# A cosformer attention and Sinkhorn-routed experts kernel: another order for the first batch, the second and third batch's attention, and the loads and transposes

## The chip, the cores and the metric

The kernel runs on one core of a Trainium2 chip. The metric is the device time of one execution in microseconds. Three executions of the kernel before took 971.24, 970.00 and 970.04 us, so the median is 970.04 us. The one that was profiled is the first of them.

The core has a matrix engine (PE; its weight loads are listed as PEld), a vector engine (DVE), a scalar engine (ACT), a general engine (POOL), and SP, which here only issues DMAs. Each engine works through its own list in order. DMAs are issued by POOL (loads that change float32 to float16 on the way) and by SP (transposes and the saved sums).

## The reference

Attention with cosine weights on 8 batches of 8 heads, 576 positions, head size 64, and then 8 experts on the 4608 rows that this gives:

```python
q_p = phi(q, cos_w, sin_w)              # relu, times cos and times sin, side by side
k_p = phi(k, cos_w, sin_w)
kv = einsum('bhsf,bhsd->bhfd', k_p, v)  # per head: features x head size
z = sum(k_p, axis=2)
num = einsum('bhsf,bhfd->bhsd', q_p, kv)
den = einsum('bhsf,bhf->bhs', q_p, z)[..., None] + 1e-06
x = (num / den) as 4608 rows of 512

P = exp(x @ w_gate - max)
for _ in range(8):                      # Sinkhorn
    P /= P.sum(1) + 1e-09; P /= P.sum(0) + 1e-09; P *= N / E
for e in range(8):
    out += P[:, e:e+1] * (relu(x @ w1[e]) @ w2[e])
```

## The kernel before, in words

The program has two phases. The second phase (expert 0's last tiles with the Sinkhorn iterations between them, then experts 1 to 7 by a scheme of seven products on quarter matrices) is the same in both kernels. The change lies in the first phase, which computes attention for all 8 batches and, interleaved with it, expert 0's two layers for the first 7 blocks of 512 rows.

**Order.** The lists of PE, DVE and ACT are written out by hand: te, ve and se are wrappers that tie each instruction behind the last one of the same engine. So an instruction that waits holds all that stand behind it. A block j has 16 slots: slots 0 to 7 are layer 1 (`ffn1`, one group of four matmuls of 512 columns and a relu on ACT each), slots 8 to 15 are layer 2 (`ffn2`, four matmuls each; every second one ends with a copy to the accumulators). `at(j, slot, fn, ...)` hangs a step of attention behind a slot. In block j these are the steps that finish batch b = j + 1 and those that prepare batch b + 1.

**Steps of a batch**, each for hk = 0 to 3 (two heads at a time):

- `load(b, half, names)`: POOL issues one load of 288 KB per name and half (two hk). The pool `ld` has 4 buffers a name, so two batches fit.
- `prep_q`: DVE's relu (from batch 2 on) and product with cos and sin give q_p, in a buffer of `qp_pool`. From batch 2 on SP then issues a DMA transpose of q_p into q_pT. For batches 0 and 1 `turn` transposes on PE by matmuls with the identity, and ACT or DVE moves the result out of PSUM with a relu.
- `prep_k` (relu on ACT or DVE), `prep_kp` (product with cos and sin on DVE), `prep_v` (copy of v next to a column of ones, on DVE or ACT); `prep_kv` is the last two.
- `sums(b, half)`: 36 small matmuls give kv and the key sums z for two hk, then ACT copies kv out and DVE writes `zsel`. Batch 0 gets its key sums apart, by `key_sums`, before the products k_p are there.
- `denominators(b)`: 24 matmuls of q_pT with zsel, then on DVE reciprocal, hi and hl.
- `spread_out(b, hk)`: three matmuls spread hl over the partitions, ACT copies them out as rb. `numerators(b, hk)`: four matmuls, and DVE's product with rb gives xT, the rows that the experts read. `attend` is both. The four PSUM banks of `small_ps` are shared by turns, sums, spread_out and numerators.
- `gates(b)`: 16 or 20 small matmuls and an exponential on ACT.

**Gates of the DMAs.** A load with `held_back` waits for the last DVE instruction that stands in the program before it; with `behind=(b, hk)` it waits instead for the transpose of that batch and hk to land. In the other direction the transposes of batches 3 and 4 wait for the landing of the first half of v of their batch, those of batches 5 to 7 for the second half of k.

**The start.** While the first loads land PE runs matmuls on constants (`idle_ps`), and `keep_busy(n)` puts n x 128 columns more of them between the steps of batch 0. Batch 0's steps are written out in order by hand; with their last ones layer 1's first four groups (`first_l1`) are interleaved by k-tile.

Of the kernel before, what the change touches and what calls it, by code (L numbers as in the profile page):

```python
# [10 lines left out]
FP32 = mybir.dt.float32  # L11
# [14 lines left out]
def kernel(  # L26
# [185 lines left out]
    with ExitStack() as p1:  # L212
        ld = p1.enter_context(tc.tile_pool(name="ld", bufs=4))
        kp_pool = p1.enter_context(tc.tile_pool(name="kp_pool", bufs=4))
        qp_pool = p1.enter_context(tc.tile_pool(name="qp_pool", bufs=4))
        qT_pool = p1.enter_context(tc.tile_pool(name="qT_pool", bufs=1))
        kv_pool = p1.enter_context(tc.tile_pool(name="kv_pool", bufs=2))
        rb_pool = p1.enter_context(tc.tile_pool(name="rb_pool", bufs=3))
# [8 lines left out]
        turnings = {}  # L227
        sources = {"q": q, "k": k, "v": v}

        def load(b, half, names="qkv", held_back=False, behind=None):  # L230
            for name in names:
                x = ld.tile([P, 2, C, D], F16, name=f"{name}_ld")
                view = sources[name][b].rearrange("(hk hh) (p c) d -> (hh p) hk (c d)", hh=2, c=C)
                i = nc.gpsimd.dma_start(
                    out=x[:].rearrange("p hk c d -> p hk (c d)"),
                    in_=view[:, 2 * half : 2 * half + 2],
                )
                if behind is not None:

                    after(turnings[behind], i)  # L240
                elif held_back:

                    after(ve.last, i)
                landing[name, b, half] = i
                for i in range(2):
                    loaded[name, b, 2 * half + i] = x[:, i]
# [6 lines left out]
        load(0, 1, "q")  # L253
# [6 lines left out]
        load(0, 0, "k")  # L260
# [7 lines left out]
        load(0, 1, "k")  # L268
        for half in range(2):
            load(0, half, "v")  # L270
# [22 lines left out]
        for _ in range(110):  # L293
            te.matmul(
                out=idle_ps[:, 0:HP], lhsT=ones_sq[:],
                rhs=ones_sq[:, 0:1].to_broadcast([P, HP]), start=True, stop=True,
            )
# [17 lines left out]

        def halve():
            for hh in range(2):
                ve.tensor_copy(
                    out=cs_half[hh * HP : (hh + 1) * HP, :, :, hh],
                    in_=cs[hh * HP : (hh + 1) * HP, :, :, 0],  # L320
                )

# [6 lines left out]
        for h in range(H):  # L329
            ve.memset(zmask[:, h, h : 32 : H], 1.0)  # L330
        C3 = C // 3
        ones_col = const.tile([P, 1], FP32, name="ones_col")
        ve.memset(ones_col[:], 1.0)
        ones_all = const.tile([P, P], FP32, name="ones_all")
        ve.memset(ones_all[:], 1.0)
        eps_row = cs_pool.tile([1, 32], FP32, name="eps_row")
        ve.memset(eps_row[:], 1e-6 / XS)

        lent = acc_lo[:, G_LO - 4 : G_LO, :].rearrange("p g d -> p (g d)").bitcast(F16)
        VA = C * (D + 2)  # L340
        v_augs = [
            lent[:, i * VA : (i + 1) * VA].rearrange("p (c d) -> p c d", d=D + 2)
            for i in range(4)
        ]
        for t in v_augs:
            ve.memset(t[:, :, D : D + 1], 1.0 / XS)
# [18 lines left out]
        )  # L365
        wg_ld = cs_pool.tile([P, KT, E], FP32, name="wg_ld")
# [6 lines left out]

        q_pTs = [qT_pool.tile([P, C, P], F16, name=f"q_pT{i}")[:] for i in range(6)] + [
# [5 lines left out]
        ]  # L380
        def prep_k(b, hk, by_scalar=True):
            k16 = loaded["k", b, hk]
            if b and by_scalar:
                se.activation(out=k16, in_=k16, func=AF.Relu)
            else:
                ve.tensor_scalar(out=k16, in0=k16, scalar1=0.0, scalar2=None, op0=ALU.max)

        def prep_q(b, hk):
# [12 lines left out]
            if by_dma:  # L401
# [5 lines left out]
                if b >= 3:  # L407

                    after(landing["v", b, 0] if b < 5 else landing["k", b, 1], turned)
                turnings[b, hk] = turned  # L410
# [78 lines left out]
        def sums_begun(b, half, banks=(ps_s, "small_ps")):  # L489
# [7 lines left out]
            kv_ps = [banks[0].tile([P, 512], FP32, name=banks[1]) for hh in range(2)]  # L497
# [157 lines left out]
        for hk in range(HK):  # L655
            prep_q(0, hk)
            if hk == 1:
                halve()
            if hk == 3:
                prep_k(0, 0)  # L660
                prep_k(0, 1)
                z_ps = key_sums(0)
            for i in range(3):
                turn(0, hk, i, True)
                keep_busy(3 * (hk < 3))
        prep_kp(0, 0)
        key_sums_made(0, z_ps)
        for hk in (2, 3):
            prep_k(0, hk)
        prep_kp(0, 1)  # L670
        denominators(0, range(0, 4))
        z_ps = key_sums(1)
        keep_busy(4)
        key_sums_made(1, z_ps)
        prep_kp(0, 2)
        denominators(0, range(4, 8))
        prep_kp(0, 3)
        sums_made(0, 0, sums_begun(0, 0))
        keep_busy(20)
        spread_out(0, 0)  # L680
        numerators(0, 0)
        keep_busy(4)
        spread_out(0, 1)
        sums_made(0, 1, sums_begun(0, 1, (ps_h[0], "h_ps")))
# [7 lines left out]

        def first_l1(kt, fts):
            for ft in fts:
                te.matmul(
                    out=first_ps[ft][:],
                    lhsT=w0[0][:, kt, ft * P : (ft + 1) * P],
                    rhs=xT[:, kt, 0:TCH],
                    start=(kt == 0),
                    stop=(kt == KT - 1),  # L700
                )
                if kt == KT - 1:
                    se.activation(out=hT[:, ft, 0:TCH], in_=first_ps[ft][:], func=AF.Relu)

        numerators(0, 1)
        spread_out(0, 2)
        first_l1(0, (2, 3, 0, 1))
        numerators(0, 2)
        spread_out(0, 3)
        first_l1(1, range(4))  # L710
        numerators(0, 3)
        prep_k(1, 0)
        prep_k(1, 1)
        first_l1(2, range(4))
        first_l1(3, range(4))
        for hk in range(HK):
            if hk >= 2:
                prep_k(1, hk, False)
            prep_kp(1, hk)
# [3 lines left out]
        for j in range(B):  # L723
            b = j + 1
            if j == 0:
# [4 lines left out]
                for hk in range(HK):  # L730
                    for i in range(3):
                        at(0, (6, 6, 7, 7)[hk], turn, 1, hk, i, i != 1)
                    if hk == 0:
                        at(0, 6, prep_q, 1, 3)
                    if hk in (1, 3):
                        for i in (hk - 1, hk):
                            at(0, (6, 7)[hk // 2], prep_v, 1, i, ve.tensor_copy)
# [6 lines left out]
            elif b < B:  # L744
                if j == 1:
# [12 lines left out]
                    at(j, 5, sums, b, 1)  # L758
                else:
# [4 lines left out]
                at(j, 6 if j == 1 else 4, denominators, b)  # L764
# [18 lines left out]
            elif b + 1 < B:  # L783
                for slot, fn, hk in (
                    (4, prep_q, 0), (5, prep_q, 1), (9, prep_k, 0), (8, prep_q, 2),
                    (10, prep_k, 1), (12, prep_q, 3), (12, prep_k, 2), (13, prep_k, 3),
                    (13, prep_kv, 0), (14, prep_kv, 1),
                ) if j == 1 else (
                    (5, prep_q, 0), (6, prep_q, 1), (8, prep_k, 0), (8, prep_q, 2),
                    (9, prep_k, 1), (10, prep_q, 3), (10, prep_k, 2), (11, prep_k, 3),  # L790
                    (11, prep_kv, 0), (14, prep_kv, 1),
                ):
                    at(j, slot, fn, b + 1, hk, *((se.copy,) if fn is prep_v else ()))
            if j == 1:
                for name in "qkv":
                    for half in range(2):
                        at(j, 12, load, b + 2, half, name, True, (b + 1, 1))
            elif j and b + 2 < B:
                for half in range(2):
                    at(j, 11 + half, load, b + 2, half, "qkv", True, (b + 1, 1))  # L800
# [519 lines left out]
```

## Time and profile before

| | |
|---|---|
| median of three executions | 970.04 us |
| the profiled execution | 971.24 us |
| its span, first to last instruction | 969.5 us |
| granted clock of PE | 0.999 |
| first phase's blocks 1 to 6 begin at | 43.98, 64.51, 83.59, 102.60, 121.50, 140.50 us |
| mean time of one DVE product q_p or k_p (128x1152) | 0.75 us |
| a relu of layer 1 on ACT (128x512) | 0.60 us |
| a copy of v on DVE, on ACT (128x576) | 0.45, 0.66 us |
| four matmuls of 512 columns, back to back | 0.86 us |

A line of a timeline has the start, the duration, the engine, the source line, the operation, output and inputs, shape and type, how often, and in brackets the idle time ahead of it with what ended it. A line of stretches has the stretch, its length, PE's busy time with the number of its instructions, PE's granted clock, the DMA engines' busy share, and GB/s. A line of DMA issues has output and input, the queue, the operation, how often, size, and the time from issue to landing.

### The profile page before, as it was taken

The numbers are of one execution on the slowest core, as the hardware profiler recorded it, in microseconds if no ns is written. First come the engines' busy times: TensorE is split into PE (matmuls) and PEld (weight loads), VectorE is DVE, ScalarE is ACT, GpSimd is POOL, SyncE is SP. The second block draws the span as 40 slices with busy tenths as digits, with TensorE's granted clock in tenths as the row PEclk, the third lists the DMA queues.
The fourth block names the chain that finished last, engine by engine and source line by source line (L and its number), as shares of the span: only waits on it lengthen the run. The fifth ranks groups of instructions, "written<-read, shape, count | busy, mean of one in ns | idle before, by whom it ended". The sixth has DMA issues, their size and how long they took to land.

```text
span 969.5 us, 20321 instructions
## 1 busy us (share of the span) xinstructions
PE 958.3 (99%) x7886; PEld 673.5 (69%) x7886; DVE 809.1 (83%) x1834; ACT 564.7 (58%) x1261; POOL 60.4 (6%) x82
## 2 busy tenths in 40 slices
PE   8999999999999999999999999999999999999997
PEld 6545555567777777777777777777777777777775
DVE  6877776889888888988898888987888987987886
ACT  5767665577776555555555555555555555555551
POOL 6231300010000000000000000000000000000001
PEclk9999999999999999999999999999999999999999
DMA  9999978240013311331004301331004301014445
GB/s 166 182 169 168 167 122 185 45 85 34 25 41 77 69 35 40 69 72 47 26 25 94 68 26 50 69 66 52 26 25 94 68 26 49 26 34 127 118 91 122
DMA packets 81200, 74.72 MB, mean 77 GB/s; under 512 B 33360, under 2 KB 73040, under 8 KB 81104
## 3 DMA queue, kind: packets, MB, share of 16 engines
q0 software_dynamic: 27232, 30.94, 20.5%
q1 hardware_dynamic: 53632, 42.24, 17.6%
q8 instruction: 61, 1.00, 0.4%
q14 instruction: 35, 0.29, 0.1%
q10 hardware_dynamic: 240, 0.26, 0.1%
HBM read 84.30 MB, written 12.98 MB: 100 GB/s over the span
## 4 chain that ended last, share of the span: by engine, by line
PE 91%; DMA 4%; issue 2%; DVE 2%; POOL 1%; ACT 0%; POOLq 0%; ACTq 0%; SPq 0%; DVEq 0%
PE rows_ps L109 34%; PE h_ps L109 28%; PE p_ps L109 11%; PE copied_ps L109 11%; PE y_ps L109 4%; PE small_ps L109 3%; DMA w1e<-in_moe_w_dram 1%; DMA w2e<-in_moe_w_dram 1%; DMA k_ld<-in_k_dram 1%; DMA q_ld<-in_q_dram 1%; DVE acc_hi L987 0%; POOL hs_last L1002 0%; DMA out_dram<-acc_lo 0%; DVE acc_lo L987 0%; DVE den L109 0%
## 5 line engine op out<-in xcount | busy, mean ns | idle before, releaser
L987 DVE SCALAR_TENSOR_TENSOR acc_lo<-rows_ps,P_tok,acc_lo 128x512 f32<-128x512 f32 (+1 forms) x322 | 203.6, 641 | 76.0 <-PE rows_ps L109 75.9
L109 PEld LDWEIGHTS <-H 128*128 128x128 f16 x2080 | 203.1, 98 | 82.3 <-issue 1.4
L923 ACT CAST u<-h_ps 128x384 f16<-128x384 f32 x288 | 137.5, 478 | 130.1 <-PE h_ps L109 130.1
L109 PEld LDWEIGHTS <-w1e 128*128 128x128 f16 x1632 | 158.0, 98 | 67.5 <-issue 4.7
L917 DVE CUSTOM_DVE_ANT_0 H<-p_ps,u 128x384 f16<-128x384 f32 x329 | 181.4, 551 | 7.7 <-PE p_ps L109 7.0
L109 PEld LDWEIGHTS <-hs 128*128 128x128 f16 x1500 | 146.6, 98 | 56.2
L109 PE MATMUL h_ps<-S,w1e 128*128 128x384 f16 x672 | 164.1, 326 | 1.0 <-ACT u L923 0.6
L109 PE MATMUL p_ps<-xT,T 128*128 128x384 f16 x672 | 164.1, 326 | 0.2
L109 PE MATMUL rows_ps<-V,H 128*128 128x256 f16 x1000 | 150.0, 273 | 0.7 <-DVE acc_hi L987 0.7
L109 PE MATMUL rows_ps<-w2e,hs 128*128 128x256 f16 x1000 | 150.0, 273 | 0.0
L109 PE MATMUL h_ps<-xT,w1e 128*128 128x384 f16 (+1 forms) x616 | 148.6, 350 | 0.1
L955 ACT ACTIVATE H<-h_ps 128x384 f16<-128x384 f32 x144 | 70.6, 490 | 94.5 <-PE h_ps L109 94.5
L109 PEld LDWEIGHTS <-T 128*128 128x128 f16 x1008 | 98.5, 98 | 30.4 <-issue 3.2
L109 PE MATMUL rows_ps<-w2e,H 128*128 128x256 f16 (+1 forms) x568 | 94.4, 285 | 0.0
L936 ACT COPY copied_ps<-h_ps 128x384 f32<-128x384 f32 x144 | 67.5, 469 | 35.8 <-PE h_ps L109 35.2
L946 ACT ACTIVATE H<-copied_ps 128x384 f16<-128x384 f32 x144 | 70.8, 492 | 20.4 <-PE copied_ps L109 20.4
L109 PE MATMUL h_ps<-S,T 128*128 128x384 f16 x336 | 81.8, 324 | 0.3
L109 PE MATMUL copied_ps<-xT,w1e 128*128 128x384 f16 x336 | 82.1, 326 | 0.0
L109 PE MATMUL copied_ps<-w2e,H 128*128 128x256 f16 x504 | 75.5, 272 | 0.0
L109 PE MATMUL rows_ps<-V,hs 128*128 128x256 f16 x500 | 74.9, 272 | 0.0
L987 DVE SCALAR_TENSOR_TENSOR acc_lo<-copied_ps,P_tok,acc_lo 128x256 f32<-128x256 f32 x126 | 60.2, 478 | 0.6 <-PE copied_ps L109 0.2
L987 DVE SCALAR_TENSOR_TENSOR acc_hi<-rows_ps,P_tok,acc_hi 128x512 f32<-128x512 f32 (+1 forms) x56 | 41.3, 738 | 19.9 <-PE rows_ps L109 19.1
(151 smaller groups left out, 942.3 us busy)
## 6 DMA issues: line engine op xcount, KB each, us to landing
S<-x_saved SPq DMA_DIRECT2D x114, 192.0 KB, 2.4
out_dram<-acc_lo SPq DMA_DIRECT2D x62, 128.0 KB, 2.4
w1e<-in_moe_w_dram POOLq DMA_DIRECT2D x7, 1024.0 KB, 8.8
w2e<-in_moe_w_dram POOLq DMA_DIRECT2D x7, 1024.0 KB, 9.6
q_ld<-in_q_dram POOLq DMA_DIRECT2D x16, 288.0 KB, 6.8
k_ld<-in_k_dram POOLq DMA_DIRECT2D x16, 288.0 KB, 8.1
v_ld<-in_v_dram POOLq DMA_DIRECT2D x16, 288.0 KB, 9.3
x_saved<-S SPq DMA_DIRECT2D x12, 192.0 KB, 1.8
```

The lines of the kernel that those rows point to most:

```text
L109: i = getattr(self.engine, name)(*args, **kwargs)
L917: latest = ve._custom_dve(TENSOR_ADD_SAT, out=out, in0=ps[:, 0:TU], in1=t[:], s0=FP32_MAX, s1=0.0)
L923: se.copy(out=t[:], in_=ps[:, 0:TU])
L936: se.copy(out=Y[:, 0:TU], in_=X[:, 0:TU])
L946: se.activation(out=h11, in_=Y[:, 0:TU], func=AF.Relu)
L955: se.activation(out=h12, in_=X[:, 0:TU], func=AF.Relu)
L987: ve.scalar_tensor_tensor(out=a, in0=rows, scalar=P_tok[:, g, self.e : self.e + 1], in1=a, op0=ALU.mult, op1=ALU.add,)
```

## The change

What it does, part by part:

1. Pools: `qp_pool` has 3 buffers in place of 4, `rb_pool` 4 in place of 3.
2. Gates of the DMAs: no load waits for a transpose any more; all the later ones wait for DVE's last instruction. Of the transposes only that of batch 3, hk 0 waits, for the second half of v to land.
3. The start: POOL makes its two constants between the first and the second load of q; cs_half is filled before the first q_p; the other constants move behind; 74 matmuls of 128 columns in place of 110 of 64.
4. Batch 0: the fourth q_p stands behind the first key relus, the product k_p of the second pair ahead of the second key relus; both sums stand together ahead of spread_out; spread_out and numerators of one hk follow each other, with one k-tile of layer 1's four groups behind each; batch 1's k steps are spread between them. The fillers are dealt otherwise.
5. Batch 1 (block 0): turns at slots 5, 6, 6, 7 in place of 6, 6, 7, 7; two of the four copies of v are on ACT.
6. Blocks 1 to 6: steps on k and v of the next batch stand at other slots, mostly earlier; the first sums of batch 3 move to the last slot of block 1, the second to the first slot of block 2, and batch 3's denominators to slot 3.

```diff
-        qp_pool = ...(tc.tile_pool(name="qp_pool", bufs=4))
+        qp_pool = ...(tc.tile_pool(name="qp_pool", bufs=3))
-        rb_pool = ...(tc.tile_pool(name="rb_pool", bufs=3))
+        rb_pool = ...(tc.tile_pool(name="rb_pool", bufs=4))
...
-                if behind is not None:
-                    after(turnings[behind], i)
-                elif held_back:
+                if held_back:
                     after(ve.last, i)
...
-        for _ in range(110):
-            te.matmul(out=idle_ps[:, 0:HP], ...)
+        for _ in range(74):
+            keep_busy(1)
...
-                if b >= 3:
-                    after(landing["v", b, 0] if b < 5 else landing["k", b, 1], turned)
-                turnings[b, hk] = turned
+                if b == 3 and hk == 0:
+                    after(landing["v", b, 1], turned)
...
         for hk in range(HK):
-            prep_q(0, hk)
-            if hk == 1:
-                halve()
             if hk == 3:
                 prep_k(0, 0)
                 prep_k(0, 1)
                 z_ps = key_sums(0)
+                prep_q(0, hk)
+                key_sums_made(0, z_ps)
+            else:
+                prep_q(0, hk)
             for i in range(3):
                 turn(0, hk, i, True)
-                keep_busy(3 * (hk < 3))
+                keep_busy(3)
         prep_kp(0, 0)
-        key_sums_made(0, z_ps)
-        for hk in (2, 3):
-            prep_k(0, hk)
-        prep_kp(0, 1)
-        denominators(0, range(0, 4))
-        z_ps = key_sums(1)
-        keep_busy(4)
-        key_sums_made(1, z_ps)
-        prep_kp(0, 2)
-        denominators(0, range(4, 8))
-        prep_kp(0, 3)
-        sums_made(0, 0, sums_begun(0, 0))
-        keep_busy(20)
-        spread_out(0, 0)
-        numerators(0, 0)
-        keep_busy(4)
-        spread_out(0, 1)
-        sums_made(0, 1, sums_begun(0, 1, (ps_h[0], "h_ps")))
+        prep_kp(0, 1)
+        denominators(0, range(0, 4))
+        keep_busy(8)
+        for hk in (2, 3):
+            prep_k(0, hk)
+        z_ps = key_sums(1)
+        prep_kp(0, 2)
+        key_sums_made(1, z_ps)
+        prep_kp(0, 3)
+        keep_busy(5)
+        denominators(0, range(4, 8))
+        for half in range(2):
+            sums_made(0, half, sums_begun(0, half))
+            keep_busy((0, 18)[half])
...
-        numerators(0, 1)
-        spread_out(0, 2)
-        first_l1(0, (2, 3, 0, 1))
-        numerators(0, 2)
-        spread_out(0, 3)
-        first_l1(1, range(4))
-        numerators(0, 3)
-        prep_k(1, 0)
-        prep_k(1, 1)
-        first_l1(2, range(4))
-        first_l1(3, range(4))
-        for hk in range(HK):
-            if hk >= 2:
-                prep_k(1, hk, False)
-            prep_kp(1, hk)
+        for hk in range(HK):
+            attend(0, hk)
+            for kt in ((), (0,), (1,), (2, 3))[hk]:
+                ...
+            for i in ((), (0,), (1, 2), ())[hk]:
+                prep_k(1, i, i < 2)
+            for i in ((), (0,), (1,), (2, 3))[hk]:
+                if i == 3:
+                    prep_k(1, i, False)
+                prep_kp(1, i)
...
-                        at(0, (6, 6, 7, 7)[hk], turn, 1, hk, i, i != 1)
+                        at(0, (5, 6, 6, 7)[hk], turn, 1, hk, i, i != 1)
...
-                            at(0, (6, 7)[hk // 2], prep_v, 1, i, ve.tensor_copy)
+                    if hk == 2:
+                        at(0, 6, prep_v, 1, 0, se.copy)
+                        at(0, 6, prep_v, 1, 2, ve.tensor_copy)
+                    if hk == 3:
+                        at(0, 7, prep_v, 1, 1, se.copy)
+                        at(0, 7, prep_v, 1, 3, ve.tensor_copy)
...
+                elif j == 2:
+                    at(j, 0, sums, b, 1)
...
-                at(j, 6 if j == 1 else 4, denominators, b)
+                at(j, 6 if j == 1 else 3 if j == 2 else 4, denominators, b)
...
-                    (4, prep_q, 0), (5, prep_q, 1), (9, prep_k, 0), (8, prep_q, 2),
-                    (10, prep_k, 1), (12, prep_q, 3), (12, prep_k, 2), (13, prep_k, 3),
-                    (13, prep_kv, 0), (14, prep_kv, 1),
+                    (4, prep_q, 0), (5, prep_q, 1), (8, prep_k, 0), (8, prep_q, 2),
+                    (9, prep_k, 1), (10, prep_kv, 0), (10, prep_k, 2), (12, prep_q, 3),
+                    (12, prep_kv, 1), (12, prep_k, 3), (13, prep_kv, 2), (14, prep_kp, 3),
+                    (14, prep_v, 3),
                 ) if j == 1 else (
-                    (5, prep_q, 0), (6, prep_q, 1), (8, prep_k, 0), (8, prep_q, 2),
-                    (9, prep_k, 1), (10, prep_q, 3), (10, prep_k, 2), (11, prep_k, 3),
+                    (4, prep_q, 0), (5, prep_k, 0), (5, prep_q, 1), (6, prep_k, 1),
+                    (8, prep_q, 2), (8, prep_k, 2), (10, prep_q, 3), (10, prep_k, 3),
+                    (11, prep_kv, 0), (14, prep_kv, 1),
+                ) if j == 2 else (
+                    (3, prep_k, 0), (4, prep_k, 1), (5, prep_q, 0), (6, prep_q, 1),
+                    (7, prep_k, 2), (8, prep_q, 2), (10, prep_q, 3), (10, prep_k, 3),
                     (11, prep_kv, 0), (14, prep_kv, 1),
...
+                if j == 1:
+                    at(j, 15, sums, b + 1, 0)
...
-                        at(j, 12, load, b + 2, half, name, True, (b + 1, 1))
+                        at(j, 12, load, b + 2, half, name, True)
...
-                    at(j, 11 + half, load, b + 2, half, "qkv", True, (b + 1, 1))
+                    at(j, 11 + half, load, b + 2, half, "qkv", True)
```

## The prediction

> **What bounds the kernel now.** I read the page's busy shares and its chain first, then stretches of the first phase block by block, then DVE's and ACT's timelines where a block is long, then single transfers.
>
> ```profile
> PE 958.3 (99%) x7886; PEld 673.5 (69%) x7886; DVE 809.1 (83%) x1834; ACT 564.7 (58%) x1261; POOL 60.4 (6%) x82
> ...
> PE 91%; DMA 4%; issue 2%; DVE 2%; POOL 1%; ACT 0%; POOLq 0%; ACTq 0%; SPq 0%; DVEq 0%
> ```
> ```profile
> 43.98:64.51 20.53, 20.11 (x210) 1.00 1.11 156
> 64.51:83.59 19.08, 19.06 (x205) 1.00 1.05 174
> 83.59:102.60 19.01, 19.01 (x210) 1.00 1.00 168
> 102.60:121.50 18.90, 18.90 (x206) 1.00 0.95 161
> ```
>
> TensorE bounds: 11 us of 969.5 are idle. The second fence has blocks 1 to 4 (stretch, its length, PE busy): from block 2 on a block takes 18.9 to 19.1 us with PE full; block 1 takes 1.5 us more. So no reordering behind 64 us can win over 0.2 us a block; it can only open gaps. To gain or lose are the first 64 us. There the edit acts on three stretches, shown by DVE's rows (first two) and ACT's (third and fourth), then DVE's again:
>
> ```profile
> 10.65 0.53 DVE L109 TENSOR_SCALAR k_ld<-k_ld 128x576 f16<-128x576 f16 x2 [0.88 <-DMA k_ld<-in_k_dram]
> ...
> 14.40 1.35 DVE L109 RECIPROCAL den<-y_ps 96x192 f32<-96x192 f32 x1
> ```
> ```profile
> 30.27 0.87 ACT L109 ACTIVATE acc_lo<-small_ps 128x384 f16<-128x384 f32 x2
> 31.01 1.04 ACT L109 ACTIVATE acc_hi<-small_ps 128x384 f16<-128x384 f32 x2
> ```
> ```profile
> 51.61 0.31 DVE L109 TENSOR_SCALAR q_ld<-q_ld 128x576 f16<-128x576 f16 x1 [1.50 <-DMA q_ld<-in_q_dram]
> 51.95 0.76 DVE L109 TENSOR_TENSOR q_p<-q_ld,acc_hi 128x1152 f16<-128x1152 f16 x1
> 52.63 0.35 DVE L109 TENSOR_TENSOR zsel<-acc_hi,small_ps 128x64 f16<-128x64 f16 x2
> ```
>
> The first fence: batch 0's keys land at 10.6 us and 3.75 us later DVE starts the denominators' reciprocal, which all of batch 0's numerators wait for. The last: DVE stood 1.50 us for a load, and the zsel behind it, whose input was ready, waited with it. An early entry in an engine's list that waits for a DMA holds all behind it.
>
> Transfers, by windows around one issue: a transpose on SP takes 3.3 us when no load streams (issue at 60.1), 5.9 inside the start's loads (38.3) and 7.7 beside one load (43.9), whose own time was 7.4 where another of the same size took 4.7 (50.1):
>
> ```profile
> q_ld<-in_q_dram POOLq DMA_DIRECT2D x1, 288.0 KB, 7.4
> q_pT<-q_p SPq DMA_TRANSPOSE x1, 7.7
> ```
> ```profile
> q_pT<-q_p SPq DMA_TRANSPOSE x1, 3.3
> ```
>
> **Part 1: start and batch 0 (0 to 24 us).** Constants: cs_half's copies (0.54) come before q_p, and with ones, eps and the v_aug memsets all ahead of it, q_p(0,0) starts near 6.6, not 6.09. The warm-up goes from 110 matmuls of 64 columns to 74 of 128. The trace has 53 ns spacing for 64 columns up to 5.1 us and 31 after; 128 columns take 107 before (37 of them by 5.1 us) and, like the transposes of 128, 56 after: 37 x 56 = 2.1, end 7.2 instead of 6.2. Both cost nothing: the cover is the wait for keys at 10.6 (0.88 us DVE idle); the 27 transposes with fillers take 3 us and ACT's 9 evictions 3.56, so all is done by 11.5, when a hk 3 turn is next. Cover gone, the price is at most 0.6. The q load issued 0.6 later on POOL is hidden: its predecessor moves until about 4.4 us.
>
> What isn't covered: q_p(0,3), k_p(0,0) and k_p(0,1) now stand before the second key pair. DVE from 10.65, start to start: key relus 0.44, q_p 0.70, zsel 0.32, two k_p 1.40, relus 0.44, k_p 0.70, zsel 0.29, k_p 0.70 = 4.99, so the reciprocal starts near 15.7: **+1.3**. hl follows the reciprocal by 2.1 (16.08 + 0.41 - 14.40), so it is ready at 17.8 instead of 16.5. PE gets there at the same time: from the last zsel at 15.1, denominators 0.51, both sums 1.3 and fillers 1.0 end at 17.9.
>
> Then attend(0,hk) with one layer-1 group each, without spread_out a step ahead. Per hk: spread 0.42, ACT copies 0.70, numerators 0.44, DVE product 0.82, layer 1 0.86. hk 0 has no layer 1 beside it and takes 1.9, waiting for copies and banks; hk 1 to 3 take 1.7 each with k_p between DVE's products. With a last wait for DVE's product the layer-1 groups end near 25.3 against 24.1 (17.9 + 1.9 + 3 x 1.7 + 0.4): the +1.3 is kept. The old order had a sum of 0.7 in this stretch too, so the new one loses by its waits what it has less to do.
>
> **Part 2: rest of block 0 (24 to 33).** Turns of batch 1 start at slot 5, not 6, and two v copies go from DVE (0.42) to ACT (0.66 by the rows at 46.4 and 48.1). The turn at slot 6 waited 0.4 for q_p in before; now q_p is ready first, a gain of 0.4. But ACT from layer 1's relus on has 8 relus at 0.55, 8 turns at 0.41, 2 copies at 0.64: 9.0 us without a gap from 24.8, end 33.8, where the old one ended turns at 32.05. The second sums of batch 1 wait for that v copy, PE reaches slot 8 near 35.0 against 32.9: block 0 is **+2.1** (1.3 if ACT's copies fit in gaps, 2.4 with every row unoverlapped).
>
> **Part 3: blocks 1 and 2.** Three edits meet. (a) prep_k(3,0) stands at slot 8 on ACT, ahead of the eviction at 56.19 and of rb; k(3,0) lands at 50.86 + 6.3 = 57.2. ACT stands till then, rb comes 1.6 later, spread_out(2,1) waits for its bank: 0.9 to 1.3 on PE. (b) The gate is now v(3,1)'s landing, 52.99 + 8.5 = 61.5, on transpose (3,0) alone, and qp has 3 buffers: q_p(3,3) needs the buffer that this transpose reads. With 3.3 us, q_p(3,3) can't start before 64.85; it ran at 62.42. In DVE's order stand behind it k_p(3,1) and v (1.15), the product of attend(2,3) (0.82), k_p and v (3,2) (1.15), k_p(3,3) (0.75): v(3,1) ends 66.8, the last 69.4. (c) sums(3,0) is now at block 1's last slot, sums(3,1) behind block 2's first. PE ends slot 15 at 64.5, waits to 66.85, ends the sums 69.75 and slots 1 and 2 (1.75) at 71.5; the old order had the same work done at 68.65: **+2.85**. (a) lies inside this wait.
> (d) In the built order SP takes transpose (3,1) before (3,0), so it goes out at 54.0 inside the loads. The loads end later by at least 0.5 (the stream at 40 us lost that) and at most 2.7 (7.4 - 4.7); I take 0.8, near the first, since a running stream is the nearer case: total **+3.6**. Below nothing is no end here: nothing in (d) frees DMA time.
>
> **Part 4: blocks 2 to 6.** Loads wait for DVE's last, not for a transpose; transposes go as q_p is ready. Loads go 2.3 us earlier (16.2 instead of 18.5 into the block), behind the fourth transpose's issue, as the load at 82.97 did at no visible cost. k(b+1) then lands 3.7 into the next block and slot 3's ACT relu wants it at 4.8: cover 1.1. If transposes push it by 2.7, ACT stands 1.6 and PE about 1.0 a block, three or four blocks: ends 0 and +4. I take 0. qp 3 buffers for x_sums_early: those transposes landed 20 us before. rb 4 buffers: no cost.
>
> [...]
>
> **Sum.** 2.1 + 3.6 + 0 = 5.7 us. The profiled execution took 971.24 us (span 969.5 and 1.7 around it), 1.2 over the median 970.04. On the median: 975.7.
>
> **Rivals.** B: the chain of part 3 doesn't bind, since part 1's delay lets the loads finish ahead of PE; then only the start counts, 970.04 + 2.1 = 972.1. Against: these loads are issued off DVE's own work at 49.8, so they move with the block. C: loads and transposes collide in every block: 975.7 + 3 = 978.7; for it the 7.7 row, against it the calm one at 82.97. D, not slower: the start's backlog of loads (to 43 us) drains 2 us earlier against PE, so q(3,0) takes 4.7 instead of 7.4 and DVE's 1.50 us wait goes. That is 1.5 off; it decides if batch 0's reorder costs under 1.5 and (b) under nothing, i.e. the transposes land before 62.4: 968.6 to 970.0. That the edit doesn't do what it says is excluded by the built order.
>
> **How the numbers follow.** 0.2% or 1.9 us is what can be told. A (forecast) 0.63, its own range 973.5 to 978.5 (parts 1 and 2 at 1.3 to 2.4, part 3 at 2.2 to 5.5, 0.5 of part 4); B 0.12, C 0.20, D 0.05. Low end 972.0 is B, high end 980.0 C with its upper half. Within 0.2%: five hundredths of B, two of D: 0.07. Faster: 0.03.
>
> **What would show it.** The reciprocal near 15.7; ACT without gaps 25 to 34 and slot 8 near 35; block 1 or 2 with 3 to 4 us of PE waits, named after DVE's v and k_p, and q_p(3,3) waiting for a transpose; blocks 3 to 6 at 19.0. I'd be wrong if q_p(3,3) doesn't wait, if blocks 3 to 6 grow, or if batch 0's reciprocal is at 14.4.

## The result, and the profile after

The changed kernel takes 974.21 us (median of four executions, 973.68 to 974.99), the kernel before 970.44 us in the executions made beside it (970.00 to 971.24). The ratio is 1.0039, with a 95% interval of 1.0021 to 1.0056: slower, by 3.8 us where 5.7 were forecast. The profiled execution took 974.54 us, its span is 972.8 us; against the profiled execution of before that is 3.3 us more.

The page's busy shares and the chain that ended last, for the changed kernel:

```profile
PE 960.3 (99%) x7855; PEld 675.3 (69%) x7855; DVE 807.7 (83%) x1831; ACT 565.0 (58%) x1264; POOL 60.7 (6%) x82
...
PE 93%; DMA 3%; DVE 2%; ACT 1%; POOL 1%; issue 0%; POOLq 0%; DVEq 0%; SPq 0%; ACTq 0%
```

In what follows a load is named by its batch and half, as q(3,0), a step or a transpose by its batch and hk, as q_p(3,3).

PE is still the bound. Where it stands is told by the stretches of blocks 1 to 4 (stretch, its length, PE busy):

```profile
45.10:66.94 21.84, 21.10 (x245) 1.00 1.04 146
66.94:87.36 20.42, 18.93 (x173) 1.00 1.15 175
87.36:106.39 19.03, 19.03 (x209) 1.00 0.92 157
106.39:125.33 18.94, 18.94 (x206) 1.00 1.00 158
```

Blocks 3 and 4 are as long as they were (19.01 and 18.90 before). Block 2's first slot starts with the first sums of batch 3 already done, so the boundary between the first two lines is not at the same work as before; fixed places in PE's list show it better. The table has the time at which PE gets there in the two profiled executions, the difference between them, and by how much the difference grew since the row above:

| place | before | after | difference | grew by |
|---|---|---|---|---|
| first keys landed | 10.62 | 10.59 | -0.03 | |
| block 0, layer 2 starts (slot 8) | 32.90 | 34.02 | +1.12 | +1.12 |
| block 1, slot 10 | 57.15 | 57.52 | +0.37 | -0.75 |
| block 1, slot 11 | 58.74 | 60.10 | +1.36 | +0.99 |
| block 2, slots 0 to 2 and both sums of batch 3 done | 68.64 | 71.11 | +2.47 | +1.11 |
| block 2, slot 5 (batch 3's denominators done) | 71.25 | 74.83 | +3.58 | +1.11 |
| block 3 starts | 83.59 | 87.36 | +3.77 | +0.19 |

Behind it little moves: block 7 is 3.9 us late, the last matmul and the last DVE instruction 3.8 us. The spans differ by 3.3 only, because what follows the last matmul took 4.60 us in the profile of before and 4.06 here. Each step of the table but the last has its lines.

The start, by DVE's timeline. Keys land at 10.6 as before, the reciprocal starts at 15.62 (14.40 before):

```profile
10.61 0.53 DVE L109 TENSOR_SCALAR k_ld<-k_ld 128x576 f16<-128x576 f16 x2 [1.69 <-DMA k_ld<-in_k_dram]
...
15.62 1.35 DVE L109 RECIPROCAL den<-y_ps 96x192 f32<-96x192 f32 x1
```

Block 0, by ACT's timeline: from layer 1's first relus on ACT has no gap (no row between the first and the last shown has idle time ahead of it), and the last v copy ends at 33.0, right behind the last turns:

```profile
24.57 1.09 ACT L109 ACTIVATE hT<-h_ps 128x512 f16<-128x512 f32 x2 [1.13 <-PE h_ps L109]
...
31.53 0.92 ACT L109 ACTIVATE acc_hi<-small_ps 128x384 f16<-128x384 f32 x2
32.27 0.73 ACT L109 COPY acc_lo<-v_ld 128x576 f16<-128x576 f16 x1
```

Block 1, by DVE's timeline: for the load of q(3,0) it waits 0.18 us where it waited 1.50, for v(3,0), whose copy now comes earlier, 0.56, and for a transpose ahead of q_p(3,3) 0.96 where it did not wait:

```profile
51.40 0.31 DVE L109 TENSOR_SCALAR q_ld<-q_ld 128x576 f16<-128x576 f16 x1 [0.18 <-DMA q_ld<-in_q_dram]
...
62.23 0.45 DVE L109 COPY acc_lo<-v_ld 128x576 f16<-128x576 f16 x1 [0.56 <-DMA v_ld<-in_v_dram]
...
64.71 0.76 DVE L109 TENSOR_TENSOR q_p<-q_ld,acc_hi 128x1152 f16<-128x1152 f16 x1 [0.96 <-DMA q_pT<-q_p]
```

ACT's timeline has the relu of k(3,0) at slot 8, which holds the PSUM copy and rb's two copies behind it for 1.62 us:

```profile
57.45 0.68 ACT L109 ACTIVATE k_ld<-k_ld 128x576 f16<-128x576 f16 x1 [1.62 <-DMA k_ld<-in_k_dram]
58.04 0.57 ACT L109 COPY acc_lo<-y_ps 128x512 f32<-128x512 f32 x1
58.50 0.70 ACT L109 COPY rb<-small_ps 128x384 f32<-128x384 f32 x2
```

PE's timeline in block 2: the sums of batch 3 wait for DVE, and the denominators wait 0.94 us for the batch's last transpose:

```profile
68.31 0.46 PE L109 MATMUL small_ps<-acc_lo,k_p 64*128 64x65 f16 x18 [0.33 <-DVE acc_lo L109]
68.98 0.46 PE L109 MATMUL small_ps<-acc_lo,k_p 64*128 64x65 f16 x18 [0.21 <-DVE k_p L109]
...
73.68 0.35 PE L109 MATMUL small_ps<-acc_hi,zsel 128*32 128x192 f16 x6 [0.94 <-DMA acc_hi<-q_p]
```

And the DMAs behind two of these waits, by windows around their issue (the last number is the time from issue to landing). The first window is at 53.8 us, where SP sends the transpose of (3,1) beside the last load of batch 3; the second at 66.9, where the transpose of (3,3) goes out 0.1 us behind batch 4's first load:

```profile
v_ld<-in_v_dram POOLq DMA_DIRECT2D x1, 288.0 KB, 8.8
q_pT<-q_p SPq DMA_TRANSPOSE x1, 10.7
```
```profile
q_ld<-in_q_dram POOLq DMA_DIRECT2D x1, 288.0 KB, 5.7
acc_hi<-q_p SPq DMA_TRANSPOSE x1, 6.7
```

Before, the transpose of (3,3) left 0.96 us ahead of that load and took 3.2 us. The transpose of (3,1) then waited for a landing of v and went out with the others.

### The profile page after: what moved, and what is told of

The parts are those of the page before. It is cut to its first block, busy times and chain, and to the rows that moved or that the text cites. A ratio compares the mean times of both kernels' runs of the same rounds, so it can differ in the third digit from the quotient of the medians.

```text
span 972.8 us, 20259 instructions
## 1 busy us (share of the span) xinstructions
PE 960.3 (99%) x7855; PEld 675.3 (69%) x7855; DVE 807.7 (83%) x1831; ACT 565.0 (58%) x1264; POOL 60.7 (6%) x82
## 4 chain that ended last, share of the span: by engine, by line
PE 93%; DMA 3%; DVE 2%; ACT 1%; POOL 1%; issue 0%; POOLq 0%; DVEq 0%; SPq 0%; ACTq 0%
PE rows_ps L109 34%; PE h_ps L109 28%; PE p_ps L109 11%; PE copied_ps L109 11%; PE y_ps L109 5%; PE small_ps L109 3%; DMA q_pT<-q_p 1%; DMA k_ld<-in_k_dram 1%; DMA acc_hi<-q_p 1%; ACT hT L109 0%; DVE acc_hi L975 0%; ACT acc_lo L109 0%; POOL hs_last L990 0%; DMA out_dram<-acc_lo 0%; DVE acc_lo L975 0%
```

## The experiments

All times stand against executions of the kernel before on the same chip in the same session; their medians were 970.15, 970.37 and 970.50 us for the three groups below. In the diffs "-" is the kernel that the heading names.

### First group: one part of the change undone at a time

**The buffer counts back** (in the changed kernel):

```diff
-qp_pool ... bufs=3        -rb_pool ... bufs=4
+qp_pool ... bufs=4        +rb_pool ... bufs=3
```

> The changed kernel with qp_pool at 4 and rb_pool at 3 buffers again, all else as changed. Theory W (the delay of blocks 1 and 2 is a chain: the last q_p of batch 3 waits 0.96 us for a buffer that a transpose reads, and the sums of batch 3 wait for what stands behind it on DVE): q_p(3,3) starts near 63.8 instead of 64.71, the sums' wait shrinks by up to 1.0, and the kernel takes 973.2 (between 972.9 and 973.6). Rival T (transposes and loads in each other's way set the time; the buffer only shows who waits): the wait moves to the denominators of batch 3, whose last transpose still lands near 73.6, and the time stays at 974.2 within 0.4.

Measured: 980.51 us, ratio 1.0087 (1.0059 to 1.0115), but its nine times fall in two groups: three from 972.0 to 973.6 and six from 980.5 to 983.6. Neither theory had that. The profiled execution is the fastest of the nine. DVE no longer waits for a transpose ahead of q_p(3,3) (its timeline), so that wait was due to the third buffer:

```profile
63.74 0.30 DVE L109 TENSOR_SCALAR q_ld<-q_ld 128x576 f16<-128x576 f16 x1
64.08 0.76 DVE L109 TENSOR_TENSOR q_p<-q_ld,acc_hi 128x1152 f16<-128x1152 f16 x1
```

From slot 15 of block 1 to slot 3 of block 2, sums included, PE takes 5.19 us (65.29 to 70.48), against 6.10 in the changed kernel and 5.00 before: 0.9 us of the 1.1 go with the buffer counts. In this execution the last transpose of batch 3 left 0.32 us ahead of the first load of batch 4 and took 5.3 us, and PE did not wait for it.

**The gates of before back** (in the changed kernel): transposes of batches 3 and 4 wait for the first half of v, later loads for a transpose.

```diff
-if b == 3 and hk == 0:
-    after(landing["v", b, 1], turned)
+if b >= 3:
+    after(landing["v", b, 0] if b < 5 else landing["k", b, 1], turned)
+turnings[b, hk] = turned
...
-at(j, 12, load, b + 2, half, name, True)
+at(j, 12, load, b + 2, half, name, True, (b + 1, 1))
```

> The changed kernel with the DMA gates of before (loads behind the second transpose, transposes of batches 3 to 7 behind a landing), all else as changed. Theory W: q_p(3,3) still has to wait, since with 3 buffers the transpose it waits for goes out at v's landing near 61.3 and lands near 64.7, as now; so the sums still wait 1.1 and only the denominators' wait of 0.9 goes: 973.2. But the k relus at slots 3 to 6 of blocks 2 to 5 then meet loads that start 2 us later and hold ACT: plus 0 to 1 a block, so 973.2 to 976. Theory T: the transposes take 3.3 us again, all waits of block 2 go: 971.9 plus the same 0 to 3.

Measured: 973.02 us, 1.0029 (1.0018 to 1.0039), where the first theory had 973.2 to 976. The transpose of (3,3) now leaves 0.97 us ahead of the first load, takes 3.3 us, and PE's wait of 0.94 us for it is gone:

```profile
acc_hi<-q_p SPq DMA_TRANSPOSE x1, 3.3
```

The wait of q_p(3,3) stays (its buffer is read by the first transpose, 61.25 to 64.55, and it starts at 64.64). So with three buffers the gates of before do not help that wait, and the two costs are separate.

**The step tables of blocks 1 to 6 back** (in the changed kernel, with its gates and buffers):

```diff
-(4, prep_q, 0), (5, prep_q, 1), (8, prep_k, 0), (8, prep_q, 2),
-(9, prep_k, 1), (10, prep_kv, 0), (10, prep_k, 2), (12, prep_q, 3), ...
+(4, prep_q, 0), (5, prep_q, 1), (9, prep_k, 0), (8, prep_q, 2),
+(10, prep_k, 1), (12, prep_q, 3), (12, prep_k, 2), (13, prep_k, 3), ...
...
-at(j, 15, sums, b + 1, 0)
```

> The changed kernel with the step tables of blocks 1 to 6 as before (k relus later, batch 3's sums together at slot 2 of block 2, denominators at slot 4), gates, pools and first batch as changed. Theory W: ACT's wait of 1.6 us for k(3,0) goes and with it 1.0 on PE; q_p(3,3) still waits for a transpose until 64.6, DVE ends batch 3's k and v steps near 70.4, the sums wait up to 1.5 for it: 972.7 (972.2 to 973.5). Theory T: with the transposes as late as now, the denominators wait as well: 973.5 to 974.2.

Measured: 982.31 us, 1.0126 (1.0111 to 1.0140), 8 us more than the changed kernel and against both theories. Nearly all of it follows from one wait on PE's timeline, 8.27 us where the changed kernel has 0.94:

```profile
81.03 0.51 PE L109 MATMUL small_ps<-acc_hi,zsel 128*32 128x192 f16 x6 [8.27 <-DMA acc_hi<-q_p]
```

The transpose it waits for left at 66.42, behind two loads of batch 4 (65.27 and 65.98), and landed at 80.99: 14.6 us for a transfer that takes 3.3 alone. Behind the wait PE works at about half its speed for some 3 us: the first four matmuls of layer 1 take 1.82 us (from 81.54) where four of layer 2 take 0.86 further on (from 86.00), and slots 5 to 8 take 4.36 us (81.47 to 85.83) instead of 3.25; in return the sums of batch 3 are done 0.85 us sooner. That made the order of SP's last transpose and POOL's first load the new suspect.

**The start and batch 0 back** (in the changed kernel):

```diff
-            if hk == 3:
-                prep_k(0, 0)
-                prep_k(0, 1)
-                z_ps = key_sums(0)
-                prep_q(0, hk)
...
+            prep_q(0, hk)
+            if hk == 1:
+                halve()
```

> The changed kernel with the start and batch 0 in the order of before, all else as changed. The start costs 1.1 us at block 0's fifth group of layer 1 (25.22 against 24.12), so if it adds to the rest: 973.1. Theory R (the later start let the start's loads drain, so that DVE's wait for q(3,0) in block 1 fell from 1.50 to 0.18 us, which gave 0.75 back): that wait returns to some 1.5, and the time is 973.85 (973.6 to 974.1).

Measured: 974.34 us, 1.0041 (1.0029 to 1.0053): no gain, where the theories had 973.1 and 973.85. Slot 8 of block 0 moves from 34.02 to 33.74, but only because the first keys landed 0.55 us sooner in this execution; counted from there it comes later, at 23.70 against 23.43. DVE does not wait for q(3,0) in this trace, so theory R fails. And the last transpose of batch 3, which now leaves 0.04 us behind the first load, takes 8.3 us, for which PE waits:

```profile
74.49 0.34 PE L109 MATMUL small_ps<-acc_hi,zsel 128*32 128x192 f16 x6 [2.49 <-DMA acc_hi<-q_p]
```

### Second group: one part done alone

**The new start and batch 0 alone, and block 0's table alone** (both in the kernel before; the diff is that of the table, whole).

```diff
-at(0, (6, 6, 7, 7)[hk], turn, 1, hk, i, i != 1)
+at(0, (5, 6, 6, 7)[hk], turn, 1, hk, i, i != 1)
 if hk == 0:
-    at(0, 6, prep_q, 1, 3)
-if hk in (1, 3):
-    for i in (hk - 1, hk):
-        at(0, (6, 7)[hk // 2], prep_v, 1, i, ve.tensor_copy)
+    at(0, 5, prep_q, 1, 3)
+if hk == 2:
+    at(0, 6, prep_v, 1, 0, se.copy)
+    at(0, 6, prep_v, 1, 2, ve.tensor_copy)
+if hk == 3:
+    at(0, 7, prep_v, 1, 1, se.copy)
+    at(0, 7, prep_v, 1, 3, ve.tensor_copy)
```

> The kernel before with the new start and batch 0 alone (order of the first loads, warm-up, constants, batch 0's steps up to the first layer-1 groups). Theory of the prediction (F): the reciprocal starts 1.3 us later (near 15.7), the layer-1 groups of block 0 end 1.1 to 1.3 us later and the delay is kept: 971.3. Theory from the run with the old start put back (M), where slot 8 of block 0 moved by 0.28 us only: slot 8 near 33.2 instead of 32.90, and DVE's wait of 1.50 us for q(3,0) gets shorter by what block 0 got longer: 970.1 to 970.4, no wait elsewhere.

> The kernel before with block 0's step table of the changed one alone (turns of batch 1 from slot 5, two v copies on ACT). F: at most 0.8 us, slot 8 at 33.7, kept: 970.9. M: with the old start this table had cost 0.84 us at slot 8 (33.74 against 32.90) in the run with the old start put back, so 33.7 here too, but DVE's 1.50 us wait for q(3,0) in block 1 takes up some 0.75 of it: 970.1 to 970.4.

Measured: 971.43 us, 1.0008 (0.9999 to 1.0016), and 970.78 us, 1.0006 (0.9997 to 1.0015). Neither is told from no change by its time, so the traces must speak. The first keys land at another time in each execution (9.91 to 10.72 us in the thirteen traces), and everything behind them moves along; so the table counts from that landing to two places:

| start | block 0's table | reciprocal starts | block 0, slot 8 |
|---|---|---|---|
| old | old (before) | 3.78 | 22.28 |
| new | old | 5.10 | 23.35 |
| old | new | 3.78 | 23.64 |
| new | new (after) | 5.03 | 23.43 |

The new start costs 1.25 to 1.3 us at the reciprocal and 1.1 at slot 8. The new table alone costs 1.4, on top of the new start 0.1. Other traces with the same first 33 us bear this out, but scatter: three with the old start and table have slot 8 at 22.21, one with the old start and the new table at 23.70, five with both new at 23.29 to 23.63. With the old start the turn that now stands at slot 5 waits for its input (PE's timeline of that run):

```profile
26.31 0.68 PE L109 MATMUL small_ps<-ident,q_p 128*128 128x128 f16 x9 [1.08 <-DVE q_p L109]
```

The costs of the two parts do not add: 1.1 and 1.4 alone, 1.0 to 1.4 together.

**The relus of k(3,0) and k(3,1) one slot later** (in the changed kernel):

```diff
-(8, prep_k, 0), ... (9, prep_k, 1),
+(9, prep_k, 0), ... (10, prep_k, 1),
```

> The changed kernel with block 1's first two k relus of batch 3 back at slots 9 and 10 (ACT no longer waits for k at slot 8). F: the prediction's (a) lies inside the wait for q_p(3,3), which still can't start before the transpose (3,1) lands near 64.6: 974.2, unchanged; ACT's wait of 1.6 us at 57.4 is gone and PE's wait between slot 10 and 11 (1.0 us) with it, but the first sums wait by as much longer. M: (a) adds on its own: 973.2. C (collisions): the last transpose of batch 3 and the first loads of batch 4 are 0.1 us apart in the changed kernel; with DVE earlier by up to 1 us the loads go first and the transpose lands after them: 978 to 983 in some or all executions.

Measured: 974.58 us, 1.0040 (1.0027 to 1.0053): unchanged, as F said. ACT's wait falls to 0.28 us, and PE reaches slot 11 at 59.26, 1.0 us sooner counted from slot 10. But the sums end at 71.24 (71.11 in the changed kernel): PE waits elsewhere for what DVE does late.

```profile
63.46 0.54 PE L109 MATMUL small_ps<-q_pT,kv_sb 128*64 128x384 f16 x4 [0.47 <-DVE xT L109]
...
66.69 0.46 PE L109 MATMUL small_ps<-acc_lo,k_p 64*128 64x65 f16 x18 [0.47 <-DVE acc_lo L109]
```

**The changed gates alone** (in the kernel before, the reverse of the gate diff above):

> The kernel before with the changed gates alone (transpose (3,0) waits for v(3,1), the other transposes for nothing, loads of batch 4 and later for DVE's last instruction and for no transpose). F: only (d) of the prediction counts, loads and a transpose slow each other by some 0.8 us, in part hidden: 970.0 to 970.9. C (collisions decide by order): transpose (3,1) goes out inside the loads, v(3,1) lands near 62.9, SP then issues the three others 1.4 us apart, the last near 65.7, while the loads of batch 4 go near 64.4 to 65.4, ahead of it; a transpose behind two loads took 14.6 us in the run with the old step tables instead of 3.3: 978 to 981, the denominators of batch 3 waiting some 8 to 10 us for it in block 2's slot 4.

Measured: 982.20 us, 1.0126 (1.0111 to 1.0141). C is right in place and 1.2 us short in size, F's (d) far off. SP sends (3,1) at 52.42 inside batch 3's loads; it lands at 63.10 and v(3,1) at 62.53; the gated transpose leaves at 62.55, and batch 4's loads, which wait for DVE alone, start at 62.48. The transposes of (3,2) and (3,3) leave at 64.09 and 67.39 and take 14.25 and 11.90 us. The line of DMA issues around the first of them, PE's timeline, and PE's stretches behind its wait (the number behind the count is the granted clock):

```profile
k_ld<-in_k_dram POOLq DMA_DIRECT2D x1, 288.0 KB, 8.8
acc_lo<-q_p SPq DMA_TRANSPOSE x1, 14.2
```
```profile
78.38 0.51 PE L109 MATMUL small_ps<-acc_lo,zsel 128*32 128x192 f16 x6 [8.29 <-DMA acc_lo<-q_p]
79.33 0.51 PE L109 MATMUL small_ps<-acc_hi,zsel 128*32 128x192 f16 x6 [0.44 <-DMA acc_hi<-q_p]
```
```profile
79.30:82.00 2.70, 2.67 (x27) 0.50 0.00 0
82.00:84.50 2.50, 2.50 (x10) 0.50 0.00 0
84.50:87.00 2.50, 2.50 (x17) 0.97 1.01 194
```

After the 8.29 us PE runs at a granted clock of 0.50 for some 6 us: from slot 5 to slot 8 of block 2 it takes 5.46 us (79.77 to 85.23) where it takes 3.25 at full clock. Slot 5 comes 9.5 us later than in the kernel before with plain copies below (70.28), whose start is the same; so of the 11.8 us some 9.5 are there by slot 5, most of it waiting, and 2.2 follow at the low clock.

This run also has the first 50 us of the kernel before, gates aside, and DVE does not wait for q(3,0) in it (its timeline; the load took 5.5 us and not 7.4):

```profile
49.52 0.34 DVE L109 TENSOR_TENSOR zsel<-acc_hi,small_ps 128x64 f16<-128x64 f16 x2
49.78 0.30 DVE L109 TENSOR_SCALAR q_ld<-q_ld 128x576 f16<-128x576 f16 x1
```

PE reaches slot 10 of block 1 at 56.15, 1.0 us sooner than in the profile of before, 0.8 counted from the keys' landing. So that profile, of the execution of 971.24 us, holds a collision which this one does not have; in none of the other twelve traces does this load take over 6.5 us.

### Third group: the transposes' own part

Each of the 24 transposes becomes a plain copy of the same bytes on the same queue, with the order of all engines' lists unchanged; in the kernel before, in the changed one, and in the kernel before with the changed gates.

```diff
-out=qTs[b, hk], in_=q_p[:].rearrange("p c a d -> p (c a d)"),
-transpose=True,
+out=qTs[b, hk], in_=q_p[:].rearrange("p c a d -> p c (a d)"),
```

> The kernel before with each of the 24 transposes on SP replaced by a plain copy of the same 288 KB into the same tile, on the same queue with the same waits and the same order on every engine; the q tiles are left unturned, so that the numbers computed after them are other ones. A reference for the next two: 969.0 to 970.4 (a transpose that nothing waits for in the kernel before, or a few tenths that it costs the loads).

> The changed kernel with plain copies in place of the transposes. Theory T (the transposes' slowness beside loads is the price of block 2): the copy (3,1) lands some 3 to 5 us after 53.9 and q_p(3,3) no longer waits, nor do the denominators; the start and block 0 (1.36) and ACT's wait for k(3,0) (1.0) stay: b_plain + 2.0 to 2.6. Rival Q (any transfer queued behind six loads is late, turned or not): q_p(3,3) and the denominators wait as before, b_plain + 3.5 to 4.5.

> The kernel before with the changed gates (982.2 with transposes) and plain copies. T: the copies beside batch 4's loads take 3 to 6 us instead of 12 to 14, PE's wait of 8.3 us in block 2 goes: b_plain + 0 to 1.5. Q: they still take 8 us or more and PE waits 4 us or more for acc_lo or acc_hi: b_plain + 5 to 12.

Measured: 969.87 us, 0.9994 (0.9985 to 1.0004); 972.48 us, 1.0023 (1.0014 to 1.0033); 970.68 us, 1.0009 (0.9998 to 1.0021). Against the first of them the changed kernel is 2.6 us slower, at the upper end of theory T's range, and the changed gates 0.8, within it. So with copies 2.6 of the change's 3.8 us stay, and some 1.2 are the transposes'. Two of the ten executions with the changed gates and copies took 973.5 and 975.0 us, and one of the changed kernel with copies 975.0; no such execution was profiled, so what copies lose in them is open. The gates that cost 11.8 us with transposes cost next to nothing with copies in the median, though the copies still go out behind the loads: (3,2) left at 62.44, 0.03 us behind a load, and took 5.0, (3,3) behind two of them took 5.7, and PE waited for neither. The window around the first:

```profile
q_ld<-in_q_dram POOLq DMA_DIRECT2D x1, 288.0 KB, 5.8
acc_lo<-q_p SPq DMA_DIRECT2D x1, 288.0 KB, 5.0
```

What the DMA engines did from 64 to 67 us tells the two kinds apart (queue, packets, MB, share of the engines' time; q0 has the loads, q1 SP's transfers). First with the changed gates and transposes, then with copies:

```profile
q0 software_dynamic: 266, 0.29, 66.6%
q1 hardware_dynamic: 638, 0.16, 37.5%
```
```profile
q0 software_dynamic: 207, 0.24, 70.0%
q1 hardware_dynamic: 147, 0.31, 30.0%
```

With the loads holding about two thirds of the engines' time in both, the transposes move 0.16 MB in packets of 250 bytes, the copies 0.31 MB in packets of 2.1 KB, in less of the engines' time. The small packets are seen; that they are the reason for the slowness is argued, not shown.

In the changed kernel with copies q_p(3,3) does not wait (DVE's timeline), and PE waits only 0.2 us twice in blocks 1 and 2 (its waits from 44 to 80 us: total, how often, longest):

```profile
62.14 0.45 DVE L109 COPY acc_lo<-v_ld 128x576 f16<-128x576 f16 x1 [0.85 <-DMA v_ld<-in_v_dram]
62.51 0.81 DVE L109 TENSOR_TENSOR xT<-small_ps,rb 128x384 f16<-128x384 f32 x2
63.24 0.30 DVE L109 TENSOR_SCALAR q_ld<-q_ld 128x576 f16<-128x576 f16 x1
63.58 0.76 DVE L109 TENSOR_TENSOR q_p<-q_ld,acc_hi 128x1152 f16<-128x1152 f16 x1
```
```profile
PE small_ps L109 <- ACT rb L109: 0.2, 1, 0.2
PE small_ps L109 <- DVE k_p L109: 0.2, 1, 0.2
```

The copy of (3,1), sent among batch 3's loads like the transpose, took 7.1 us where the transpose took 10.7, and so q_p's buffer was free by 60.86. This run does not test the last transpose: copies leave SP 0.6 to 0.7 us apart where transposes leave 1.4 to 1.5 apart, so the copy of (3,3) left 0.83 us ahead of batch 4's first load. For that the run with the changed gates stands.

### What the runs give together

The time that one transpose of batch 3 takes, (3,3) where no other is named, against its lead over the first load of batch 4 (issue of the load less issue of the transpose):

| run | lead, us | issue to landing, us |
|---|---|---|
| changed kernel: (3,2) | +1.39 | 3.3 |
| changed kernel, gates of before | +0.97 | 3.3 |
| before | +0.96 | 3.2 |
| before, new start alone | +0.96 | 3.3 |
| before, new block 0 alone | +0.93 | 3.2 |
| changed kernel, old step tables: (3,2) | +0.35 | 5.7 |
| changed kernel, old buffer counts | +0.32 | 5.3 |
| changed kernel, old start | -0.04 | 8.3 |
| before, changed gates: (3,0) | -0.07 | 6.9 |
| changed kernel | -0.10 | 6.7 |
| changed kernel, relus later | -0.11 | 6.6 |
| changed kernel, old step tables | -1.15 | 14.6 |
| before, changed gates: (3,2) | -1.61 | 14.2 |

With a lead of 0.9 us or more these transposes took 3.2 or 3.3 us, with 0.3 us 5.3 and 5.7, behind one load 6.6 to 8.3 (not in the order of the lead), behind two or three 14.2 and 14.6. A rival is that the transpose sent among batch 3's loads drags all that follows, whatever the order. The changed kernel's own trace speaks against it: the two transposes between that one and batch 4's loads, issued at 64.00 and 65.41, took what a transpose takes alone (a window around their issue):

```profile
q_pT<-q_p SPq DMA_TRANSPOSE x1, 3.3
acc_lo<-q_p SPq DMA_TRANSPOSE x1, 3.3
```

The gates of before kept this lead: the loads waited for the landing of the second of four transposes, and the fourth had by then been issued. The changed gates leave it to chance, and the changed step tables, by which DVE reaches the loads' mark later, save it for the most part.

Two things stay open. The two groups of times of the run with the old buffer counts, some 9 us apart, have the size of this wait, and its profile shows a lead of only 0.32 us. The granted clock points the same way: 0.994 to 0.996 over the six long executions, as in the two runs with waits of 8.3 us (0.992 to 0.996), against 0.999 and 1.000 over the three short ones. But no execution of the long group was profiled, so that cause is argued. And the changed gates with the old hold on batch 4's loads alone (behind the first gated transpose), which would test the order by itself, was not tried; nor was an earlier load of q(3,0) in the kernel before. No run here beats the kernel before with the computation whole.

## Why the prediction was right, and where it was not

The direction and the range held: slower, by block 0, block 1's k and q steps and block 2's transposes, with blocks 3 to 6 unchanged. The sum was 5.7 and the measured steps make 1.12 - 0.75 + 0.99 + 1.11 + 1.11 + 0.19 = 3.77: block 0 took 1.12 where 2.1 were forecast, part 3 3.40 where 3.6 were, and the -0.75 was in no term. That this is also the difference of the medians is chance, for the two profiled executions are 3.3 us apart, and the one of before was 0.8 us over its median. Term by term:

- **Part 1, the reciprocal near 15.7 (+1.3)**: 15.62, and 1.25 to 1.3 counted from the keys' landing. Right; the layer-1 groups at slot 4 start 1.10 late where +1.2 was forecast.
- **Part 2, "ACT ... without a gap from 24.8, end 33.8"**, slot 8 near 35.0, block 0 +2.1: the mechanism held, the size did not, and this is the term that was most in error. ACT had no gap, but it began at 24.57 and its 18 instructions took 8.4 us where I summed 9.0: a relu 0.51 us from start to start and not 0.55, a turn 0.39 and not 0.41. So its v copy was done at 33.0, and slot 8 came 1.0 us behind that and not 1.2, at 34.02. Counted from the keys' landing the new start costs 1.1 us at slot 8, where I had 1.3, and the table on top of it 0.1, where I had 0.8.
- **Rival D's relief**, the 1.50 us wait for q(3,0), was left out of the sum, and half of it came: the wait fell to 0.18 us and 0.75 us came back. That it came against this profile is partly an accident of the profile: the run with the changed gates alone has the first 50 us of before and no such wait.
- **Part 3 (a), 0.9 to 1.3 on PE, "lies inside this wait"**: 0.99, and inside, as the run with the later relus shows (974.58 against 974.21).
- **Part 3 (b), q_p(3,3) waits for a transpose until 64.85, +2.85 with (a)**: it started at 64.71, and the wait is due to the third buffer, as the run with the old counts shows. But the sums end 2.10 later and not 2.85 (0.99 + 1.11). And the transpose that it waited for was not the gated (3,0), which landed at 67.30, but (3,1), the one sent inside the loads, 10.75 us long. Of q_p's three earlier tiles only that one's transpose had landed by 64.71, so its buffer was the one reused. The number was right for a wrong reason.
- **Part 3 (d), 0.8**: 1.11, by another way. I priced transpose (3,1) slowing the loads: v(3,1) did land 9.9 us after its issue where it was 8.5. The price itself was paid at the other end, by transpose (3,3) behind the next batch's first load. My upper end for (d), 2.7, was far from what the same gates can cost: 11.8 us alone. That they cost only 1.11 here is luck: the changed tables happen to bring batch 4's loads so late that only the last transpose falls behind one, by 0.1 us. The sign "3 to 4 us of PE waits" in block 1 or 2 did not come; PE idled 0.74 us in block 1 and 1.49 in block 2.
- **Part 4, 0**: blocks 3 to 6 grew by 0.02 to 0.05 us each. Right; rival C, collisions in every block, is out. From batch 4 on the last transpose leaves 1.27 us ahead of the next batch's first load (83.47 against 84.74, and so on) and takes 3.2 to 3.6 us.

On PE's clock: behind PE's wait of 0.94 us (changed kernel) and that of 2.49 us (old start) the granted clock was 1.00. Behind the one of 8.29 us (changed gates) it was 0.50, for some 6 us of work; behind the one of 8.27 us (old step tables) PE's matmuls took about twice as long for some 3 us, 1.82 us for four where later ones took 0.86. No wait between 2.49 and 8.27 us was seen, so what such a wait would do was not shown.

On transposes: with no load in flight when it left, one took 3.2 to 3.4 us (kernel before) against 2.4 for a copy of the same 288 KB (the last of batch 3, kernel before with copies), behind one load 6.6 to 8.3 against 5.0, behind two 14.6 against 5.7. In each of these places the transpose took longer than the copy.

## What to carry to other kernels

Where two queues share the DMA engines, write down for both the time of issue of what meets, not only who waits for whom: here a transpose took 3.3 us when it left 0.9 us ahead of the loads and 14 when it left behind two or three, and a gate that looks like a mere wait was what kept the lead. A wait on a DMA in one profile may belong to that execution; see whether a second trace of the same stretch has it before its removal is counted as a gain. And parts of a change that re-order the same engines are priced together: here 1.1 and 1.4 us alone made some 1.2 together.

## What the runs showed of the hardware that was not expected

- A transpose issued behind loads did not merely queue: sent 0.1 us behind one load it took 6.7 us, behind two loads 14.6 us: by the time it landed four of the six loads had, the third and fourth of them issued after it. A plain copy behind one load took 5.0 us, behind two 5.7. Sent among batch 3's loads, a transpose took 9.5 to 10.7 us, a copy 7.1 and 7.6.
- One kernel had two groups of times some 9 us apart on the same chip (972.0 to 973.6 and 980.5 to 983.6), and nothing between; in its one profile the issues of the transpose and the load that meet are 0.32 us apart.
- The first keys land between 9.91 and 10.72 us after the first instruction, from execution to execution, and DVE's reciprocal follows by 3.78 us in all six traces with the old start.
